# Attention beside a gated squared-ReLU block: `wo` and attention's output moved in transfers of 32 partitions, with waits between transfers taken from the kernel's own draft schedule

## Chip, core and metric

The kernel runs on one NeuronCore of a Trainium2 chip. The core has five engines that each run their own stream of instructions in order: TensorE (PE, matrix products; PEld is its weight load), VectorE (DVE), ScalarE (ACT), GpSimd (POOL) and SyncE (SP, which here only issues transfers). Transfers run on the 16 DMA engines that the profile counts for a core. The metric is the device time of one execution in microseconds.

## What is computed

`x` is 2048 tokens by 512, in float32. After a layer norm two branches start from the same `xn`, and are joined at the end:

```python
xn = _layernorm(x, axis=-1)
s = _A_ref(xn, A_wqkv, A_wo)                   # attention, then @ wo
g = _silu(_B_ref(xn, B_w1, B_b1, B_w2, B_b2))  # relu(xn @ w1 + b1)**2 @ w2 + b2
return x + s * g
```

Attention has 32 heads of 16 elements. Each token looks at 8 keys: its own and those 2, 4, ... 14 tokens before it; keys ahead of the first token are masked. `wo` is 512 x 512, `w1` 512 x 1792, `w2` 1792 x 512.

## The kernel before

**Numbers.** Every product is made of three float32r products: an operand is split into a high part (ACT writes `src` as float32r) and a low part (`src` minus the high part, on DVE or POOL), and high x high, high x low and low x high are added up in PSUM (`PASSES`, line 40; `split`, line 498). So behind each loaded weight stand one ACT operation and one subtraction before TensorE may use it.

**Stages.** First come the 16 tiles of 128 tokens: norm, transposition, and the products with `wqkv`. From the fifth tile on, the transposition is a shuffle of 32-partition blocks (`shuffle`, line 788: four transfers SBUF to SBUF, the rows `turn<-turn`) and a 32 x 32 transposition on DVE. q, k and v are staged in `stg` and stored to DRAM (`store_qkv`, line 930, into `sq`, `sk`, `sv`). Then the up products with `w1` run for both halves of the tokens (`ups`, line 1136; PE rows `uX`, `uY`, `uZ`). The second half's `u` goes to DRAM (`su`) and is fetched later (`load_ut`, line 1268). Last come the down products, in four chunks `c` of 512 tokens with 14 blocks `f` of 128 hidden units each. A block is 4 token tiles x 3 passes = 12 matmuls into the four PSUM tiles `pb`. `make_h` (line 1273) squares `u` on ACT into `h` and has the low part subtracted on POOL or DVE.

**Beside them.** DVE works through attention (`attention`, line 660) in eight units `u` of 256 tokens, whose 128 partitions are 16 blocks of 16 tokens by 8 groups of 4 heads. `load_u` (line 592) fetches q, k, v of a unit; `store` (line 654) writes the unit's output to DRAM, to `so`, laid out as 8 groups x 2048 tokens x 64 elements. In the down stage `load_o` (line 1320) fetches a unit back as `oq` with four heads' groups on 32 partitions, `trans_o` (line 1329) transposes 32 x 32 blocks on DVE into `oTf`, ACT writes the high part `oT`, `lowo` (line 1338) the low part, and `out_product` (line 1341) makes the 12 matmuls `pw<-wot,oT` of a tile. `finish` joins the branches and stores.

**Weights of the down stage.** During the first chunk (`c = 0`) the kernel fetches `w2` from block 6 on (`load_w2`, line 726, `split_w2`, line 730) and `wo` (`load_wo`, line 1371, two calls with two transfers each; `split_wo`, line 1377). `rwo`, the raw `wo`, and `oTf` share the two buffers of tag `rwo`.

**Order.** The kernel is traced twice. The first trace is a draft: a list scheduler (`forward`, line 219) lays all operations on the five engines with the kernel's own costs (`price`), transfers on one common wire of `RATE` bytes per ns, which SP may run `AHEAD` (2500 ns) of (line 61). It chooses the order on every engine, and whether an operation marked `E` goes to DVE or POOL. `arrange` (line 377) keeps the best of six rounds, and in the second trace fixes that order on each engine. So a change of a transfer also moves operations elsewhere. All transfers are issued by SP. Each signals one of eight DMA semaphores in turn, and waits for the transfer that had this semaphore before, eight transfers earlier, beside what its data need. A record of an operation is made in `add` (line 153), whose line 159 issues the instruction: the profile shows nearly all as L159 (L160 after the change), and operations are told apart by tile names.

Of the kernel before, what the change touches and what calls it, by code (L numbers as in the profile page):

```python
# [11 lines left out]
F32 = mybir.dt.float32  # L12
FR = mybir.dt.float32r
AF = mybir.ActivationFunctionType
# [3 lines left out]
P = 128  # L18
S = 2048
D = 512  # L20
# [10 lines left out]
UP = 256  # L31
NU = S // UP

GR = 8
CH = D // GR
BI = 16
NB = UP // BI
WIN = BI + HALO

PASSES = ((0, 0), (0, 1), (1, 0))  # L40
# [38 lines left out]
def elements(ap):  # L79
    n = 1  # L80
    for d in ap.shape[1:]:
        n *= d
    return n


class Book:
# [66 lines left out]
    def add(self, key, name, f, a, k):  # L153
        n = len(self.ops)
        engine = key
        if key == "E":
            engine = self.plan[1][n] if self.plan else "V"
            f = getattr(f[engine], name)
        ins = f(*a, **k)  # L159
        out = k["out"] if "out" in k else a[0]  # L160
        outs = [out] + ([k["accum_out"]] if "accum_out" in k else [])
        ins_ = [*(a if "out" in k else a[1:]), *(x for i, x in k.items() if i not in ("out", "accum_out"))]
        ins_ = [x for x in ins_ if isinstance(x, bass.AP)]
        two = sum(x.space != bass.MemoryType.PSUM and elements(x) > 1 for x in ins_) > (name != "tensor_scalar")
        if key == "E":
            op = Op(n, "E", ins, {e: self.price(e, name, k, ins_, out) for e in "VG"}, True)
        elif name == "dma_start":
            moved = 4
            for d in out.shape:
                moved *= d  # L170
            op = Op(n, "S", ins, 600, moved=moved)
        else:
            op = Op(n, engine, ins, self.price(engine, name, k, ins_, out),
                    engine == "V" and two or engine == "G" and elements(out) > 1 and name != "memset")
        if self.first:
            if op.engine in self.heads:
                self.heads[op.engine].starts.append(op)
                op.waits += 1
            self.heads[op.engine] = op
        func = next((x for x in a if isinstance(x, mybir.ActivationFunctionType)), None)  # L180
        op.table = func if func in (AF.Exp, AF.Silu) else None
        op.stream = self.in_stream
        self.ops.append(op)
        if engine == "P":
            if "P" in self.last:
                self.edge(self.last["P"], op)
            self.last["P"] = op
        for x, writes in [(x, False) for x in ins_] + [(x, True) for x in outs]:
            r = self.region(x)
            if r is None:  # L190
                continue
            t, p0, p1, m = r
            writes = writes or t.space == "PSUM"
            if t not in op.tiles:
                op.tiles.append(t)
                if not t.users:
                    used = self.firsts.setdefault(t.slot, [])
                    if len(used) >= t.bufs:
                        t.behind = used[-1]
                    used.append(op)  # L200
                if t.behind not in (None, op):
                    t.behind.starts.append(op)
                    op.waits += 1
                t.users.append(op)
            kept = []
            for other, w, q0, q1, k_ in t.log:
                if (w or writes) and other is not op and p0 < q1 and q0 < p1 and m & k_:
                    self.edge(other, op)
                if not (writes and p0 <= q0 and q1 <= p1 and k_ & ~m == 0):
                    kept.append((other, w, q0, q1, k_))  # L210
            kept.append((op, writes, p0, p1, m))
            t.log = kept
        return ins
# [138 lines left out]
    def tails(self, order=None):  # L352
# [21 lines left out]
        top = max(tail)  # L374
        return [top - t for t in tail]

    def arrange(self):
        if self.plan is None:
            order, best = None, None
            for _ in range(ROUNDS):  # L380
                end, order = self.forward(self.tails(order))
                if best is None or end < best[0]:
                    best = end, [op.n for op in order], [op.given for op in self.ops]
            return best[1:]
        order = [self.ops[n] for n in self.plan[0]]
        for op in self.ops:
            op.given = self.plan[1][op.n]
        for e in "PVAGS":
            line = [op for op in order if op.given == e]
            for a, b in zip(line, line[1:]):  # L390
                self.tc.add_manual_dep(b.ins.ins, a.ins.ins.name, mybir.DependencyInfo(
                    mybir.DependencyClass.NoSync, mybir.DependencyReason.DATA), reason="order")


class Kept:
# [47 lines left out]
def trace(ctx: ExitStack, tc: tile.TileContext, plan, x, wqkv, wo, w1, b1, w2, b2, out):  # L443
# [4 lines left out]
    PE, V, A, G, E = (Recorded(book, n, e) for n, e in zip(  # L448
        "PVAGE", (nc.tensor, nc.vector, nc.scalar, nc.gpsimd, dict(V=nc.vector, G=nc.gpsimd))))
    dma = Recorded(book, "S", nc.sync).dma_start  # L450

    def pool(name, stack=ctx, after=(), **k):
        return Pool(book, stack.enter_context(tc.tile_pool(name=name, bufs=1, **k)), name, after)

    const = pool("const")
    dram = pool("dram", space=bass.MemoryType.DRAM)
# [119 lines left out]
    sq = dram.tile([GR, S, CH], F32, name="sq")  # L576
    sk = dram.tile([GR, HALO + S, CH], F32, name="sk")
    sv = dram.tile([GR, HALO + S, CH], F32, name="sv")
    so = dram.tile([GR, S, CH], F32, name="so")
    sr = dram.tile([8, P, D], F32, name="sr")  # L580
    su = dram.tile([NF, P, 2, 512], F32, name="su")

# [9 lines left out]
    def load_u(what, u):  # L592
        n = BI if what == "q" else WIN
        src = dict(q=sq, k=sk, v=sv)[what]

        t = att.tile([P, n, CH], F32, name=f"{what}{u}", tag="k" if (what, u) == ("v", NU - 1) else what)
        row = src[0, u * UP:u * UP + 1, :]
        ap = bass.AP(tensor=row.tensor, offset=row.offset, ap=[[BI * CH, NB], [src.shape[1] * CH, GR], [1, n * CH]])
        dma(t.rearrange("p i c -> p (i c)"), ap)
        return t  # L600
# [52 lines left out]

    def store(u):
        v = tiles.pop(("v", u))
        row = so[0, u * UP:u * UP + 1, :]
        dst = bass.AP(tensor=row.tensor, offset=row.offset, ap=[[BI * CH, NB], [S * CH, GR], [1, BI * CH]])
        dma(dst, v[:, :BI, :].rearrange("p i c -> p (i c)"))

    def attention():  # L660

# [75 lines left out]
    mv, means, rs, shifts, xn, xb, pTs, seen, odd = ({} for _ in range(9))  # L737
# [291 lines left out]
    for a in range(2, NT, 2):  # L1029
        n, t = {2: 2, 4: 1}.get(a, 0), a + 2  # L1030
# [273 lines left out]
    p2 = pool("p2", ctx, (px, pstg, p2a, tpool))  # L1304
# [13 lines left out]
    oqs, oTs = {}, {}  # L1318

    def load_o(u):  # L1320

        if u in oqs:
            return
        oqs[u] = p2.tile([P, UP // 64, 2, 2, CH], F32, name=f"oq{u}", tag="oq")
        for g in range(GR):
            src = so[g, u * UP:(u + 1) * UP, :].rearrange("(b p e) c -> p b (e c)", p=32, e=2)
            dma(oqs[u][32 * (g // 2):32 * (g // 2) + 32, :, g % 2].rearrange("p b e c -> p b (e c)"), src)

    def trans_o(t):
        src = p2.tile([P, 512], F32, name=f"oTf{t}", tag="rwo", bufs=2)  # L1330
        src = src.rearrange("p (g n) -> p g n", g=4)
        V.transpose(out=src.rearrange("p (g h) (b n) -> p b g h n", h=2, n=32),
                    in_=oqs[t // 2][:, :, :, t % 2].rearrange("p b g (h c) -> p b g h c", c=32))
        oTs[t] = p2.tile([P, 2, 4, P], FR, name=f"oT{t}", tag="oT", bufs=3)
        A.activation(oTs[t][:, 0], src, AF.Copy)
        seen[t] = src

    def lowo(t):
        E.tensor_sub(oTs[t][:, 1], seen.pop(t), oTs[t][:, 0].bitcast(F32))

    def out_product(t, ps, cols=slice(0, D)):
        o = oTs[t]
# [26 lines left out]
    rwo = {}  # L1369

    def load_wo(i):
        rwo[i] = p2.tile([P, 2, D], F32, name=f"rwo{i}", tag="rwo", bufs=2)
        for g in range(2):
            row = wo[64 * i + 32 * g:64 * i + 32 * g + 1, :]
            dma(rwo[i][:, g], bass.AP(tensor=row.tensor, offset=row.offset, ap=[[P * D, 4], [D, 32], [1, D]]))

    def split_wo(i):
        for g in range(2):
# [14 lines left out]
    for c in range(NCH):  # L1393
        last = c == NCH - 1
        t0 = c * TPC
        for f in range(NF):
            if c == 0 and f in (2, 3):
                load_wo(f - 2)
# [25 lines left out]
            if f >= 7:  # L1424
                load_o(c * 2)
            if f in (9, 10) and not last:
                load_r(t0 + f - 9)
            if f == 11:
                for i in range(2):
                    trans_o(t0 + i)  # L1430
            if f == 12:
                for i in range(2):
                    lowo(t0 + i)
                load_o(c * 2 + 1)
# [18 lines left out]
        else:  # L1453
# [15 lines left out]
            for j in range(2, TPC):  # L1469
                n = D // 2 if j == TPC - 1 else D  # L1470
# [28 lines left out]
```

## Time and profile before

| | us |
|---|---|
| median of three runs | 477.09 |
| the three runs | 476.09, 477.09, 477.45 |
| the profiled execution | 475.35 |
| its span in the trace | 473.6 |

Durations below are from the profiled execution. Its own time is 1.75 us longer than the span that the trace shows. How the work lies over the span can be read from the slices of the page, 40 equal ones of 11.84 us, with the busy share in tenths. The weight loads (PEld) overlap with the matmuls, so the row of PE alone tells how full TensorE is.

```profile
PE   8999999999999999999999997999999999999996
...
DVE  4987977999999998999999984899999999992213
ACT  5756968866564558468584965795249535844311
POOL 2286324336997699956453567876674566376330
...
DMA  8799899999689977641860558748894994443102
```

The first slice holds the first loads and the warm-up. Slices 0 to 10 are the products with `wqkv`; the up products run to slice 22; the down stage starts in slice 22 with `c = 0`. Moved data are 87.78 MB in all.

### The profile page before, as it was taken

What the parts mean: (1) busy time and instruction counts of PE and PEld (TensorE: products, weight loads), DVE (VectorE), ACT (ScalarE), POOL (GpSimd) and SP (SyncE); (2) the same over time, 40 slices, a digit from 0 to 9 for tenths busy, and PEclk for the clock granted to TensorE, in tenths of its full rate; (3) what the DMA queues carried; (4) which work ended last, traced back from release to release, by engine and by line L of the source; (5) the groups of instructions that cost most, each with busy time, mean ns of one, the idle gap of its engine ahead of it and who ended that gap; (6) DMA issues with size and microseconds to landing.
All of it is one profiled execution on the core that took longest, in us unless ns stands there. A gap on an engine that the chain in (4) does not pass through costs nothing.

```text
span 473.6 us, 6218 instructions
## 1 busy us (share of the span) xinstructions
PE 463.6 (98%) x2037; PEld 380.6 (80%) x2037; DVE 403.9 (85%) x341; ACT 291.7 (62%) x567; POOL 280.5 (59%) x297
## 2 busy tenths in 40 slices
PE   8999999999999999999999997999999999999996
PEld 6788888888788888888888785788888888888886
DVE  4987977999999998999999984899999999992213
ACT  5756968866564558468584965795249535844311
POOL 2286324336997699956453567876674566376330
PEclk9999999999999999999999998999999999999999
DMA  8799899999689977641860558748894994443102
GB/s 276 210 219 280 287 220 285 253 230 252 184 226 275 261 239 201 227 105 47 209 155 2 156 144 205 193 124 251 174 255 115 259 238 142 146 144 91 45 19 72
DMA packets 77901, 87.78 MB, mean 185 GB/s; under 512 B 6956, under 2 KB 59436, under 8 KB 77868
## 3 DMA queue, kind: packets, MB, share of 16 engines
q1 hardware_dynamic: 77868, 87.38, 69.4%
q8 instruction: 16, 0.26, 0.2%
q14 instruction: 17, 0.14, 0.1%
HBM read 53.75 MB, written 30.47 MB: 178 GB/s over the span
## 4 chain that ended last, share of the span: by engine, by line
PE 89%; DMA 6%; POOL 1%; ACT 1%; DVE 1%; issue 1%; SPq 0%; POOLq 0%
PE pb L159 25%; PE uX L159 16%; PE pq L159 13%; PE pm L159 12%; PE pw L159 9%; PE uZ L159 8%; DMA w2r<-in_B_w 5%; PE uY L159 4%; DMA oq<-so 2%; PE warm L159 1%; SPq L159 0%; PE pxT L159 0%; POOL h L159 0%; DVE wq L159 0%; POOL w L159 0%
## 5 line engine op out<-in xcount | busy, mean ns | idle before, releaser
L159 PE MATMUL pb<-w,h 128*128 128x512 f32 x592 | 152.1, 394 | 3.6 <-POOL h L159 3.5
L159 PEld LDWEIGHTS pb<-w,h 128*128 128x128 f32 x592 | 111.6, 190 | 29.7 <-POOL h L159 5.8
L159 DVE TENSOR_TENSOR pr<-k,qp 128x2048 f32<-128x2048 f32 x32 | 72.8, 2276 | 7.3 <-ACT qp L159 5.6
L159 DVE TENSOR_REDUCE v<-pv 128x256 f32<-128x2048 f32 x32 | 73.0, 2281 | 0.7
L159 DVE TENSOR_TENSOR pv<-v,Lp 128x2048 f32<-128x2048 f32 x32 | 72.8, 2276 | 0.6
L159 DVE TENSOR_REDUCE L<-pr 128x128 f32<-128x2048 f32 x32 | 72.7, 2273 | 0.5
L159 POOL TENSOR_TENSOR h<-ut,h 128x512 fp32r<-128x512 f32 x26 | 33.3, 1295 | 34.6 <-ACT ut L159 33.3
L159 POOL TENSOR_TENSOR h<-u,h 128x512 fp32r<-128x512 f32 (+1 forms) x32 | 33.0, 1050 | 24.1 <-ACT u L159 16.8
L159 PE MATMUL pw<-wot,oT 128*128 128x512 f32 (+1 forms) x204 | 45.5, 376 | 0.0
L159 PEld LDWEIGHTS pw<-wot,oT 128*128 128x128 f32 x204 | 36.8, 188 | 7.1
L159 DVE TENSOR_TENSOR z<-z,pw 128x512 f32<-128x512 f32 (+1 forms) x17 | 11.0, 650 | 26.2 <-ACT z L159 14.4
L159 ACT ACTIVATE ut<-ut 128x512 f32<-128x512 f32 x42 | 24.8, 624 | 12.1 <-DMA ut<-su 12.0
L159 PE MATMUL pq<-wq,XA 128*128 128x512 f32 x122 | 31.5, 391 | 0.3 <-DVE wq L159 0.3
L159 ACT ACTIVATE u<-uX,b1t 128x512 f32<-128x512 f32 x28 | 19.2, 687 | 18.2 <-PE uX L159 14.6
L159 ACT ACTIVATE h<-ut 128x512 fp32r<-128x512 f32 x28 | 16.4, 625 | 22.3 <-PE pb L159 10.5
L159 POOL TENSOR_TENSOR u<-u,more 128x512 f32<-128x512 f32 x14 | 18.2, 1297 | 17.4 <-ACT more L159 16.7
L159 POOL TENSOR_TENSOR oT<-oTf,oT 128x512 fp32r<-128x512 f32 x16 | 20.7, 1295 | 11.3 <-ACT oT L159 11.3
L159 PEld LDWEIGHTS pq<-wq,XA 128*128 128x128 f32 x122 | 22.7, 188 | 5.4 <-DVE wq L159 0.7
L159 ACT ACTIVATE stg<-pm 128x512 f32<-128x512 f32 x30 | 18.0, 599 | 14.3 <-PE pm L159 12.0
L159 ACT ACTIVATE u<-u 128x512 f32<-128x512 f32 (+1 forms) x54 | 26.4, 528 | 0.2
L159 ACT ACTIVATE stg<-pq 128x512 f32<-128x512 f32 x24 | 14.3, 598 | 13.4 <-PE pq L159 10.8
L159 ACT ACTIVATE h<-u 128x512 fp32r<-128x512 f32 (+1 forms) x36 | 17.4, 528 | 5.9 <-PE pb L159 5.8
(166 smaller groups left out, 990.4 us busy)
## 6 DMA issues: line engine op xcount, KB each, us to landing
k<-sk SPq DMA_DIRECT2D x8, 960.0 KB
v<-sv SPq DMA_DIRECT2D x8, 960.0 KB, 7.1
su<-u SPq DMA_DIRECT2D x28, 256.0 KB, 2.5
ut<-su SPq DMA_DIRECT2D x28, 256.0 KB, 4.5
x<-in_A_x SPq DMA_DIRECT2D x16, 256.0 KB, 4.9
sk<-stg SPq DMA_DIRECT2D x8, 512.0 KB, 3.3
sq<-stg SPq DMA_DIRECT2D x8, 512.0 KB, 5.0
sv<-stg SPq DMA_DIRECT2D x8, 512.0 KB, 6.0
```

The source lines that it names most:

```text
L159: ins = f(*a, **k)
```

## The change

Four things change.

*Attention's output in DRAM.* `so` becomes 8 units x 32 x 8 groups x 512: a row holds half a block (`HB` = 8 tokens) of one group, 2 KB. `store` writes a unit in two transfers, one for each half of the blocks. `load_o` fetches a unit in four transfers of 32 partitions with two groups each, in place of eight of 32 partitions with one group each. The tokens then stand in `oq` in another order; `trans_o` puts `oTf` out in that order, and `positions` writes the high and low parts of `oT` back to the old one, with a step of 4 elements.

*`wo`.* `load_wo` fetches each half in four transfers of 32 partitions (2 x 512 elements on each), in place of two of 128 partitions (512 elements on each). The old pattern on the DRAM side is 4 x 32 x 512, the new one 32 x 2 x 512.

*Waits.* `landed` goes through the transfers in the draft's order. For each it looks for the latest transfer that has landed, by the draft, when this one starts; if that is a later one than any wait so far covers, the pair is put on a list, except for the operations of the first part of the program (`early`: up to the norm of tile 2). In the second trace `arrange` makes each pair a real dependency, so that SP waits for the earlier transfer before it issues the later one.

*The order*, as the scheduler makes it anew.

```diff
+HB = BI // 2
...
+        op.early = self.first
...
+    def landed(self, order):
+
+        out, line, last = [], [op for op in order if op.moved], -1
+        for i, op in enumerate(line):
+            done = max((j for j in range(i) if line[j].end <= op.start), default=-1)
+            if done > last and not op.early:
+                out.append((op.n, line[done].n))
+                last = done
+        return out
...
+        for n, m in self.plan[2]:
+            self.tc.add_manual_dep(self.ops[n].ins.ins, self.ops[m].ins.ins.name, mybir.DependencyInfo(
+                mybir.DependencyClass.Sync, mybir.DependencyReason.DATA), reason="landed")
...
-    so = dram.tile([GR, S, CH], F32, name="so")
+    so = dram.tile([NU, UP // HB, GR, HB * CH], F32, name="so")
...
-        row = so[0, u * UP:u * UP + 1, :]
-        dst = bass.AP(tensor=row.tensor, offset=row.offset, ap=[[BI * CH, NB], [S * CH, GR], [1, BI * CH]])
-        dma(dst, v[:, :BI, :].rearrange("p i c -> p (i c)"))
+        for i in range(2):
+            dma(so[u].rearrange("(b i) g n -> i b g n", i=2)[i], v[:, HB * i:HB * (i + 1), :].rearrange("p i c -> p (i c)"))
...
-        oqs[u] = p2.tile([P, UP // 64, 2, 2, CH], F32, name=f"oq{u}", tag="oq")
-        for g in range(GR):
-            src = so[g, u * UP:(u + 1) * UP, :].rearrange("(b p e) c -> p b (e c)", p=32, e=2)
-            dma(oqs[u][32 * (g // 2):32 * (g // 2) + 32, :, g % 2].rearrange("p b e c -> p b (e c)"), src)
+        oqs[u] = p2.tile([P, 2, UP // 64, 2, CH], F32, name=f"oq{u}", tag="oq")
+        for g in range(GR // 2):
+            dma(oqs[u][32 * g:32 * g + 32].rearrange("p g b e c -> p g (b e c)"), so[u, :, 2 * g:2 * g + 2])
...
-        src = src.rearrange("p (g n) -> p g n", g=4)
-        V.transpose(out=src.rearrange("p (g h) (b n) -> p b g h n", h=2, n=32),
-                    in_=oqs[t // 2][:, :, :, t % 2].rearrange("p b g (h c) -> p b g h c", c=32))
+        V.transpose(out=src.rearrange("p (g h b n) -> p b g h n", g=2, h=2, n=32),
+                    in_=oqs[t // 2][:, :, :, t % 2].rearrange("p g b (h c) -> p b g h c", c=32))
...
-        A.activation(oTs[t][:, 0], src, AF.Copy)
-        seen[t] = src
+        seen[t] = src.rearrange("p (g b n) -> p g b n", g=4, n=32)
+        A.activation(positions(t, 0), seen[t], AF.Copy)
+
+    def positions(t, a):
+        return oTs[t][:, a].rearrange("p g (n b) -> p g b n", b=4)
...
-        E.tensor_sub(oTs[t][:, 1], seen.pop(t), oTs[t][:, 0].bitcast(F32))
+        E.tensor_sub(positions(t, 1), seen.pop(t), positions(t, 0).bitcast(F32))
...
-        for g in range(2):
-            row = wo[64 * i + 32 * g:64 * i + 32 * g + 1, :]
-            dma(rwo[i][:, g], bass.AP(tensor=row.tensor, offset=row.offset, ap=[[P * D, 4], [D, 32], [1, D]]))
+        for g in range(4):
+            rows = wo[P * g + 64 * i:P * g + 64 * i + 64, :]
+            dma(rwo[i][32 * g:32 * g + 32], rows.rearrange("(h c) n -> c h n", c=32))
```

TensorE's order is the same before and after. Three places of the other engines' orders follow.

SP at the start of the down stage of `c = 0`, before. A row names the tile written, the tile read, and the shape; `w2r7` is the raw `w2` of block 7, `so` attention's output in DRAM, `v4` and `q6` are attention's inputs, `xr` the `x` that `finish` adds.

```order
L159 DMA w2r7_2780<-in_B_w2 128x512
L159 DMA so_155<-v3_1494 16x8x1024
L159 DMA w2r8_2819<-in_B_w2 128x512
L159 DMA rwo0_2816<-in_A_wo 128x1x512 x2
L159 DMA oq0_2939<-so_155 32x4x128 x8
L159 DMA rwo1_2841<-in_A_wo 128x1x512 x2
L159 DMA w2r9_2844<-in_B_w2 128x512
L159 DMA w2r10_2864<-in_B_w2 128x512
L159 DMA v4_1539<-sv_154 128x1x1920
L159 DMA w2r11_2885<-in_B_w2 128x512
L159 DMA q6_1565<-sq_152 128x1x1024
```

The same place now:

```order
L160 DMA w2r7_2788<-in_B_w2 128x512
L160 DMA v4_1543<-sv_154 128x1x1920
L160 DMA w2r8_2829<-in_B_w2 128x512
L160 DMA rwo0_2824<-in_A_wo 32x2x512 x4
L160 DMA oq0_2951<-so_155 32x1024 x4
L160 DMA rwo1_2851<-in_A_wo 32x2x512 x2
L160 DMA w2r9_2856<-in_B_w2 128x512
L160 DMA rwo1_2851<-in_A_wo 32x2x512 x2
L160 DMA xr0_2988<-in_A_x 128x512
L160 DMA xr1_3006<-in_A_x 128x512
L160 DMA w2r10_2876<-in_B_w2 128x512
L160 DMA w2r11_2897<-in_B_w2 128x512
```

`v4` has moved ahead of `w2r8`, the two `xr` ahead of `w2r10`; the store `so` of unit 3 now lies earlier (ahead of `w2r6`).

ACT in the same stretch, before; `wot` is the high part of `wo`, `w28` that of `w2`'s blocks 8 and 9, `h0_6` the high part of `h` for blocks 6 and 7 of `c = 0`, and `u03<-u03` squares in place for the low part.

```order
L159 ACTIVATE w28_2821<-w2r8_2819 128x512
L159 ACTIVATE wot_2750<-rwo0_2816 128x512 x2
L159 ACTIVATE qp5_2_1553<-q5_1520 128x512
L159 ACTIVATE u06_2607<-u06_2607 128x2x256
L159 ACTIVATE wot_2750<-rwo1_2841 128x512
L159 ACTIVATE h0_6_2869<-u03_2454 128x512 x2
L159 ACTIVATE u03_2454<-u03_2454 128x2x256 x2
L159 ACTIVATE w28_2821<-w2r9_2844 128x512
L159 ACTIVATE w210_2866<-w2r10_2864 128x512
L159 ACTIVATE wot_2750<-rwo1_2841 128x512
L159 ACTIVATE h0_8_2915<-u04_2589 128x512 x2
```

And now:

```order
L160 ACTIVATE w28_2831<-w2r8_2829 128x512
L160 ACTIVATE wot_2758<-rwo0_2824 128x512 x2
L160 ACTIVATE qp5_2_1557<-q5_1523 128x512
L160 ACTIVATE u06_2615<-u06_2615 128x2x256
L160 ACTIVATE h0_6_2881<-u03_2462 128x512 x2
L160 ACTIVATE u03_2462<-u03_2462 128x2x256 x2
L160 ACTIVATE w28_2831<-w2r9_2856 128x512
L160 ACTIVATE wot_2758<-rwo1_2851 128x512 x2
L160 ACTIVATE w210_2878<-w2r10_2876 128x512
L160 ACTIVATE h0_8_2927<-u04_2597 128x512 x2
```

The first `wot<-rwo1` has moved from ahead of `h0_6` to behind `w28<-w2r9`.

SP some 23 transfers into the program, with what each waits for, before. `x9` is a tile of `x`, `k0` attention's first input, `turn4` the shuffle of the first pair of tiles that needs one; a DMAHW name is one of the eight DMA semaphores.

```order
L159 DMA x9_391<-in_A_x 128x512 [waits DMAHW6_49,DVE_49]
L159 DMA k0_1331<-sk_153 128x1x1920 [waits DMAHW7_49]
L159 DMA turn4_337<-turn4_337 32x4x256 [waits DMAHW0_49,DVE_49,PE_49]
L159 DMA turn4_337<-turn4_337 32x4x256 [waits DMAHW1_49]
L159 DMA turn4_337<-turn4_337 32x4x256 [waits DMAHW2_49]
L159 DMA turn4_337<-turn4_337 32x4x256 [waits DMAHW3_49]
```

Now:

```order
L160 DMA x9_391<-in_A_x 128x512 [waits DMAHW6_49,DVE_49]
L160 DMA k0_1331<-sk_153 128x1x1920 [waits DMAHW7_49,DMAHW2_49]
L160 DMA turn4_337<-turn4_337 32x4x256 [waits DMAHW6_49,DVE_49,PE_49]
L160 DMA turn4_337<-turn4_337 32x4x256 x2
L160 DMA turn4_337<-turn4_337 32x4x256 [waits DMAHW3_49]
```

`x9` is the latest transfer that used DMAHW6 there, so the shuffle's first transfer now waits for `x9` to land; two of the four have no wait of their own left.

More of the change, by code (lines that the diff above doesn't have):

```diff
@@ L382, in arrange @@
                 if best is None or end < best[0]:
-                    best = end, [op.n for op in order], [op.given for op in self.ops]
+                    best = end, [op.n for op in order], [op.given for op in self.ops], self.landed(order)
             return best[1:]
```

## Prediction

> **What bounds the kernel now.** I read the busy shares first, then TensorE's rows in the timeline, then stages, and only then the transfers. TensorE is the bound: 98% of the span, while no other engine passes 85%.
>
> ```profile
> span 473.6 us, 6218 instructions
> PE 463.6 (98%) x2037; PEld 380.6 (80%) x2037; DVE 403.9 (85%) x341; ACT 291.7 (62%) x567; POOL 280.5 (59%) x297
> ```
>
> So only time in which TensorE stands still, or runs at a lower clock, can be won. The stages show where that is (columns: window, its length, TensorE's busy us and instructions, granted clock, DMA share, GB/s):
>
> ```profile
> 90.00:100.00 10.00, 10.00 (x45) 1.00 1.13 200
> ...
> 260.00:270.00 10.00, 9.91 (x45) 1.00 0.48 145
> 270.00:280.00 10.00, 9.78 (x43) 1.00 0.39 112
> 280.00:290.00 10.00, 8.29 (x30) 0.85 1.05 218
> 290.00:300.00 10.00, 8.71 (x38) 0.98 0.84 212
> 300.00:310.00 10.00, 9.71 (x42) 1.00 0.54 169
> ```
>
> A full window holds 45 or 46. From 260 to 310 some 30 matmuls are missing; this is the first 512 tokens' down product (`c = 0`), where `w2`, `wo` and attention's output are loaded. TensorE's timeline gives the size:
>
> ```profile
> 266.65 3.49 PE L159 MATMUL pb<-w,h 128*128 128x512 f32 x13
> ...
> 272.77 3.34 PE L159 MATMUL pb<-w,h 128*128 128x512 f32 x14
> ...
> 283.65 1.01 PE L159 MATMUL pb<-w,h 128*128 128x512 f32 x3
> 286.37 7.36 PE L159 MATMUL pb<-w,h 128*128 128x512 f32 x24 [1.71 <-POOL h L159]
> 295.02 2.79 PE L159 MATMUL pb<-w,h 128*128 128x512 f32 x11 [1.29 <-POOL h L159]
> ...
> 311.87 3.34 PE L159 MATMUL pw<-wot,oT 128*128 128x512 f32 x14
> 336.51 2.72 PE pb L159 x12
> ```
>
> The last row is from the chain: 12 matmuls in 2.72 us, 0.2267 each. The stage has 14 x 4 x 3 = 168, which need 38.08 us; it took 311.87 - 266.65 = 45.22. So **7.14 us are lost**. By parts: up to 272.77, 23 matmuls (5.21) in 6.12, 0.91 lost; up to 283.65, 48 in 10.88, none; then 3 (0.68) in 2.72, **2.04**; 24 (5.44) in 8.65, **3.21**; 70 (15.87) in 16.85, **0.98**. The 3.21 is more than its stop of 1.29, because the clock was halved after the first stop, as finer windows show:
>
> ```profile
> 266.00:267.00 1.00, 1.00 (x6) 1.00 1.01 293
> 269.00:270.00 1.00, 1.00 (x6) 1.00 0.27 97
> 278.00:279.00 1.00, 1.00 (x6) 1.00 0.19 66
> 279.00:280.00 1.00, 1.00 (x6) 1.00 0.31 115
> 288.00:289.00 1.00, 1.00 (x4) 0.50 1.15 269
> ```
>
> What ended the stops is POOL's `h`; behind it stands ACT, and behind ACT a transfer. ACT's timeline, then SP's, then the chain:
>
> ```profile
> 282.73 0.63 ACT L159 ACTIVATE wot<-rwo 128x512 fp32r<-128x512 f32 x1 [4.57 <-DMA rwo<-in_A_wo]
> ...
> 289.23 0.63 ACT L159 ACTIVATE w<-w2r 128x512 fp32r<-128x512 f32 x1 [3.80 <-DMA w2r<-in_B_w]
> 266.85 1.25 SPq L159 DMA_DIRECT2D rwo<-in_A_wo  x2
> 268.14 7.94 SPq L159 DMA_DIRECT2D oq<-so  x8
> 276.24 1.13 SPq L159 DMA_DIRECT2D rwo<-in_A_wo  x2
> 277.48 1.02 SPq L159 DMA_DIRECT2D w2r<-in_B_w  x2
> 277.48 11.73 DMA w2r<-in_B_w
> 292.51 9.93 DMA w2r<-in_B_w
> ```
>
> `wo` goes out at 266.85, and at 269 the DMA engines are 27% busy at 97 GB/s, where three microseconds before they did 293; at 278 and 279, after the second pair, it is 19% and 31%. About 4 of 16 engines work. The four transfers are 1 MB, at 97 to 115 GB/s some 9 to 11 us for these few engines. The `w2` rows issued behind them at 277.48 take 11.73 us, because part of each sits behind `wo`. ACT, in order, waits first for `wo` (4.57) and then for `w2` (3.80); `h` is queued behind both. By 291 the backlog also holds up the last `w2` rows (9.93), hence the 0.98.
>
> **The change, part by part.** (1) `wo`. The DRAM side of the old pattern begins with a dimension of 4, the new one with 32. I read the 27% as "as many engines as that dimension". The nearest rows for a transfer of 32 partitions are the shuffles `turn<-turn`, alone on the rings here:
>
> ```profile
> 94.00:95.00 1.00, 1.00 (x6) 1.00 1.16 147
> ```
>
> All engines work, but at 147 GB/s, SBUF to SBUF; the 2 KB rows from HBM at 266 had 293. So 1 MB takes between 3.6 and 7.1 us instead of about 10. I take the near end, since direction and row size are those of 266.
>
> The Trainium skill, page "DMA: Bandwidth & Descriptors", section "Why a DMA increments its semaphore by 16 and not by 1", says that a transfer runs on the largest number up to 16 that divides the slowest dimension of both its patterns, so 4 before and 16 after. The 27% agrees. The same page's "Rules for kernel authors" speak against this edit: most bandwidth with 128 partitions and 1 MiB or more, and disjoint partition parts serialize, so one transfer is better. By that rule the loads would gain nothing and the time would stay; here the 128-partition load is the one at 97 GB/s.
>
> Does everything then come in time? SP's new order puts `v4` (960 KB), `w2r8`, `wo`, `oq0`, `w2r9`, `xr0`, `xr1` ahead of `w2r10`: 960 + 256 + 512 + 512 + 512 + 256 + 512 + 256 KB = 3.87 MB from about 266.5. At 293 GB/s the last is through at 279.7, at the 218 of window 280 at 284.2, and lands up to 2 us later. ACT must split `w2r10` ahead of `h0_8` (0.63 + 1.14, then 1.3 on POOL), which TensorE wants 8 x 2.72 after 267.56, at 289.3: so it must land by 286.2. It holds at either end, at the slow one just. So 2.04 + 3.21 go, and with them the 0.98: **-6.23**. The 0.91 at the start stays: ACT is busy without a break there, and its order up to that place is the same:
>
> ```profile
> 261.00:278.00 17.00, 17.00 (x38) 1.00 0.48 140
> ```
>
> One half of `h0_1`'s subtraction moves to DVE, behind a product of 2.28 us; by DVE's place then this costs or wins up to 0.9, I take 0.
>
> (2) Attention's output. Stores go from 8 of 512 KB to 16 of 256 KB, loads from 64 of 64 KB to 32 of 128 KB with rows of 2 KB for 512 B. SP issues 20 fewer in all, and SP binds nothing. Transposes stay; `oT` is now written with a step of 4 elements. No ACT or POOL row shows such a write; on DVE one with a step of 2 (`pv`) costs what one without has (`pr`):
>
> ```profile
> L159 DVE TENSOR_TENSOR pr<-k,qp 128x2048 f32<-128x2048 f32 x32 | 72.8, 2276 | 7.3 <-ACT qp L159 5.6
> ...
> L159 DVE TENSOR_TENSOR pv<-v,Lp 128x2048 f32<-128x2048 f32 x32 | 72.8, 2276 | 0.6
> ...
> L159 POOL TENSOR_TENSOR oT<-oTf,oT 128x512 fp32r<-128x512 f32 x16 | 20.7, 1295 | 11.3 <-ACT oT L159 11.3
> ```
>
> I take 0; at double price 1.3 us on POOL per tile, hidden beside TensorE except for `oT0`, queued ahead of `h0_10`: at most +1.3.
>
> (3) The added waits. An SP wait holds every transfer behind it. The sharpest place is early: `turn4` now waits for `x9`, and behind it stand the stores of q, k and v.
>
> ```profile
> 21.74 2.92 SPq L159 DMA_DIRECT2D x<-in_A_x  x4
> ...
> 28.89 2.59 SPq L159 DMA_DIRECT2D turn<-turn  x4
> 37.27 1.32 DVE L159 STREAM_TRANSPOSE pxT<-turn 128x512 f32<-128x512 f32 x2 [3.45 <-DMA turn<-turn]
> x<-in_A_x SPq DMA_DIRECT2D x16, 256.0 KB, 4.9
> su<-u SPq DMA_DIRECT2D x28, 256.0 KB, 2.5
> ```
>
> `x9` goes out last of its four, near 24.3, and lands by the median 4.9 later, 29.2: `turn4` goes 0.3 later. The rings still hold `k0`'s 960 KB then, so its bytes move when they did. A wait costs only where the rings run dry; then by the lone `su` row 2.5 - 0.9 (256 KB at 293) = 1.6 us. Below nothing it can hardly be: order in the rings stays as issued. I take **+0.3**, with 0 and 3 as ends.
>
> What is late next? DVE, with attention; its last transposes and the product that needs them:
>
> ```profile
> 437.93 1.30 DVE L159 STREAM_TRANSPOSE oTf<-oq 128x512 f32<-128x512 f32 x2 [2.78 <-DMA oq<-so]
> 464.19 5.75 PE L159 MATMUL pw<-wot,oT 128*128 128x512 f32 x36
> ```
>
> 464.19 - 439.23 - 0.6 - 1.3 = 23 us of slack, of which the gain takes 6.
>
> Sum, against the profiled execution's own time: 475.35 - 6.23 + 0.3 = 469.4. That execution lies 1.74 below the median 477.09; I carry the difference over: 477.09 - 5.93 = **471.2**.
>
> **Rivals.** *Part of it* (0.12): `w2r10` or the ones after land behind 286, since `xr` now goes first; the clock drops again and the 3.21 stays. For it: the margin at 218 GB/s. Against: the 293 of 266. 477.1 - 2.04 - 0.98 = 474.1. *The split changes nothing* (0.10): four engines were not the cause, or 32 partitions load no faster, so the stops stay; 477.1. For it only the 147 of the shuffles; against it the 16 busy engines there. *Slower* (0.06): the added waits empty the rings in the first 130 us, where each of the six pairs of tiles needs a shuffle, a DVE transpose and a split before TensorE may go on. Price 1.6 us each, 9.6 in all: 477.1 - 5.9 + 9.6 = 480.8. It decides once the pairs lose over 7.4, five of six. Against it: DMA shares above 1 there (1.13 in window 90), so work is queued when a wait ends.
>
> **How the numbers follow.** My forecast, chance 0.72, has 470.0 (the 0.91 goes too and the waits cost nothing), or 468.8 if some of the 1.74 by which the other runs are longer comes from these same stops, to 473.5 (3 for the waits, or 1.3 for `oT0` and some of DVE's 0.9). With the part case the range goes to 475.6: **468.8 to 475.6**, leaving out 0.16 and some edges. About 0.3%, 1.43 us, is what a measurement of this kernel can tell from no change. Faster: 0.72 + 0.12 = 0.84, less 0.01 of spill, 0.83. Same: 0.10 and the spill, 0.11. Slower: 0.06.
>
> **What would show it.** Right: a DMA share near 1 just after `wo` goes out; `w2` rows landing in under 8 us; no ACT wait on `rwo`; no granted clock of 0.5; 168 matmuls in under 40 us. Wrong: a stop with `w2r` behind it near `h0_8`; TensorE idle before 266, ended by `stg`, XA or SA; an `oT` operation well over 1.3 us on POOL.

## The result, and the profile after

The changed kernel took 469.52 us (median of four runs, 469.12 to 470.2) where the kernel before, with a fourth run beside the three, took 477.27 (476.09 to 478.5): a ratio of 0.9839, 95% interval 0.981 to 0.9868. The prediction was 471.2, in a range of 468.8 to 475.6. The profiled execution took 469.87, span 468.1.

The page of the changed kernel first, busy time of each engine:

```profile
span 468.1 us, 6197 instructions
PE 460.5 (98%) x2037; PEld 379.1 (81%) x2037; DVE 403.5 (86%) x345; ACT 300.8 (64%) x569; POOL 281.5 (60%) x293
```

TensorE's share is 98% as it was: a share of the span could not show the gain, since the stops were a small part of it and the slow clock of 288 counted as busy. The stages show it (changed kernel; columns as in the prediction: window, length, TensorE's busy us and instructions, granted clock, DMA share, GB/s):

```profile
260.00:270.00 10.00, 10.00 (x45) 1.00 0.78 188
270.00:280.00 10.00, 10.00 (x46) 1.00 0.90 210
280.00:290.00 10.00, 10.00 (x46) 1.00 0.68 201
290.00:300.00 10.00, 10.00 (x46) 1.00 0.89 204
300.00:310.00 10.00, 10.00 (x46) 1.00 0.62 173
...
269.00:270.00 1.00, 1.00 (x6) 1.00 0.85 177
...
288.00:289.00 1.00, 1.00 (x6) 1.00 0.47 98
```

The five windows hold 229 matmuls in place of 198. At 269, where the DMA engines were 27% busy, they are 85% busy; at 288, where the clock was halved, it is 1.00. TensorE's timeline has the size of it, and something new:

```profile
266.22 3.34 PE L160 MATMUL pb<-w,h 128*128 128x512 f32 x13
...
304.70 5.60 PE L160 MATMUL pw<-wot,oT 128*128 128x512 f32 x24
...
359.10 3.11 PE L160 MATMUL pb<-w,h 128*128 128x512 f32 x13
364.32 3.34 PE L160 MATMUL pb<-w,h 128*128 128x512 f32 x14
371.41 2.79 PE L160 MATMUL pb<-w,h 128*128 128x512 f32 x11 [0.81 <-POOL h L160]
...
458.44 5.75 PE L160 MATMUL pw<-wot,oT 128*128 128x512 f32 x36
```

The first chunk takes 304.70 - 266.22 = 38.48 us where its 168 matmuls need 38.08: 0.40 lost, not 7.14. But from there to the last `pw` it is 458.44 - 304.70 = 153.74, and it was 464.19 - 311.87 = 152.32: 1.42 us are given back in later chunks, most of it at the stop at 371. ACT's timeline says how the first chunk got through:

```profile
275.47 1.15 ACT L160 ACTIVATE wot<-rwo 128x512 fp32r<-128x512 f32 x2
...
280.89 1.16 ACT L160 ACTIVATE wot<-rwo 128x512 fp32r<-128x512 f32 x2
285.00 0.63 ACT L160 ACTIVATE w<-w2r 128x512 fp32r<-128x512 f32 x1 [2.95 <-DMA w2r<-in_B_w]
```

ACT no longer waits for `wo` (it waited 4.57). It still waits 2.95 for `w2r10`, up to 285.00: that fits, with little to spare, since the next thing on ACT is `h0_8`, which TensorE asks for at about 266.22 + 8 x 2.72 = 288.

### The profile page after: what moved, and what is told of

Read it like the earlier page. It is cut to its first block, busy times and chain, and to the rows that moved or that the text cites. A ratio compares the mean times of both kernels' runs of the same rounds, so it can differ in the third digit from the quotient of the medians.

```text
span 468.1 us, 6197 instructions
## 1 busy us (share of the span) xinstructions
PE 460.5 (98%) x2037; PEld 379.1 (81%) x2037; DVE 403.5 (86%) x345; ACT 300.8 (64%) x569; POOL 281.5 (60%) x293
## 4 chain that ended last, share of the span: by engine, by line
PE 82%; DVE 6%; DMA 6%; ACT 3%; issue 2%; POOL 2%; SPq 0%; DVEq 0%; ACTq 0%; POOLq 0%
PE pb L160 21%; PE uX L160 16%; PE pq L160 13%; PE pm L160 12%; PE uZ L160 8%; PE pw L160 6%; PE uY L160 4%; DMA oq<-so 2%; DMA k<-sk 2%; DVE v L160 1%; DVE pv L160 1%; DVE L L160 1%; PE warm L160 1%; DMA xr<-in_A_x 1%; DVE pr L160 1%
## 5 line engine op out<-in xcount | busy, mean ns | idle before, releaser
L160 PE MATMUL pb<-w,h 128*128 128x512 f32 x592 | 149.9, 390 | 0.8 <-POOL h L160 0.8
L160 POOL TENSOR_TENSOR h<-ut,h 128x512 fp32r<-128x512 f32 x24 | 30.8, 1295 | 39.1 <-ACT ut L160 31.9
L160 POOL TENSOR_TENSOR h<-u,h 128x512 fp32r<-128x512 f32 (+1 forms) x29 | 29.8, 1045 | 20.8 <-ACT u L160 17.6
L160 POOL TENSOR_TENSOR oT<-oTf,oT 128x512 fp32r<-128x512 f32 x16 | 25.1, 1571 | 6.3 <-ACT oT L160 6.3
```

## The experiments

Four theories for the gain: A, the leading dimension of 4 in `wo`'s DRAM pattern kept it on four DMA engines; B, the new order on SP and ACT; C, the added waits; D, attention's larger transfers. The stage losses below are all worked out as above: from the first `pb` of the first chunk to its first `pw`, less 38.08.

**One pattern, nothing else.** `wo_lead128` keeps every instruction of the kernel before in its place.

```diff
-            row = wo[64 * i + 32 * g:64 * i + 32 * g + 1, :]
-            dma(rwo[i][:, g], bass.AP(tensor=row.tensor, offset=row.offset, ap=[[P * D, 4], [D, 32], [1, D]]))
+            dma(rwo[i][:, g], wo[P * (2 * i + g):P * (2 * i + g) + P, :])
```

> The kernel before, with one edit: the four wo transfers read 128 consecutive rows each, so their DRAM pattern is 128 x 512 in place of 4 x 32 x 512. Size, number, place and order of all transfers and instructions stay as before; which row of wo stands on which partition changes, so attention's projection is another one. Theory A (the leading dimension of 4 kept wo on four DMA engines, and the rest queued behind it): DMA share above 0.7 just after wo goes out, in place of 0.27; the stops of 1.71 and 1.29 us are gone; 470.0 to 472.0 us. Theory B (the new order on SP and ACT is what helps): 476 to 478, stops as before. Theory C (the added waits) and theory D (attention's larger transfers): the same, 476 to 478.

Measured: 468.59 us, ratio 0.982 (0.9803 to 0.9838). Its windows just after `wo` goes out, and TensorE's timeline:

```profile
269.00:270.00 1.00, 0.97 (x4) 1.00 0.87 281
270.00:271.00 1.00, 1.00 (x5) 1.00 0.96 297
```

```profile
267.42 3.50 PE L159 MATMUL pb<-w,h 128*128 128x512 f32 x13
271.36 0.73 PE L159 MATMUL pb<-w,h 128*128 128x512 f32 x2 [0.22 <-POOL h L159]
...
306.39 5.60 PE L159 MATMUL pw<-wot,oT 128*128 128x512 f32 x24
```

The share is 0.87 at 281 GB/s where it was 0.27 at 97, and 0.89 us are lost: the small loss at the start, which no part of `wo` touches. The time is below what A expected. The whole gain is in this one pattern; B, C and D are not needed for it. That the load has 128 partitions here and 32 in the changed kernel makes no difference that these runs show.

**The parts of the change alone.** `wo_only` is the kernel before with the new `load_wo`; `waits_only` is the kernel before with `landed`; `no_waits` and `o_only` are:

```diff
-        for n, m in self.plan[2]:
+        for n, m in ():
```

that is, the changed kernel without the waits, and for `o_only` with the old `load_wo` too.

> The kernel before with the new load_wo alone (four transfers of 32 partitions); the scheduler makes its order anew; no added waits, attention's output as before. Theory A: 469.5 to 472 us, no stop in the first chunk. Theories C and D: 476 to 478. Theory B says nothing here unless the order comes out as in the changed kernel.

> The kernel before with the added waits alone (the list landed, and the dependencies it makes); the draft's order stays as before. Theory A: wo still on four engines, the stops stay, 476 to 479 us (waits cost 0 to 2). Theory C (the waits pace the rings so that w2 is not queued behind wo): 470 to 473.

> The changed kernel without the added waits; the order on every engine stays as in the changed kernel. Theory A: no stop in the first chunk, 468 to 470.5 us. If the waits are also what makes the new stop of 0.98 us at 371 (they hold up attention's transfers, DVE runs late, ACT stands at qp behind it and POOL's h comes late), that stop is gone too: 468.0 to 468.7; if ACT's doubled oT writes make it, it stays: 469 to 470. Theory C: 474 or more.

> The changed kernel with the old load_wo and without the added waits, so attention's output alone; the scheduler makes its order anew. Theory A: the stops near 286 and 295 stay, 475.5 to 478.5 us. Theory D (fewer, larger transfers of oq free the rings): 470 to 473.

| | us | ratio to before, 95% | lost in the first chunk |
|---|---|---|---|
| `wo_only` | 469.22 | 0.9828 (0.9813 to 0.9843) | 0.91 |
| `waits_only` | 477.49 | 0.9999 (0.9988 to 1.001) | 8.59 |
| `no_waits` | 470.04 | 0.9842 (0.9825 to 0.9858) | 0.40 |
| `o_only` | 475.45 | 0.9953 (0.9937 to 0.9968) | 7.19 |

`wo_only` has all of the gain, as A said (0.28 below the range expected). The waits do nothing that can be measured, alone or in the changed kernel: C falls. `o_only` keeps the stops, as A said, though its median is just below the 475.5 expected: attention's part, with the order that comes with it, is worth 0.5% beside the old `wo`, and nothing that can be measured beside the new one. That half per cent has no place in the traces, since the two profiled spans are only 0.3 us apart; the profile of the kernel before is its fastest execution, so the traces can't show it, and it stays unexplained. The timeline of `waits_only` shows that the old stops only moved:

```profile
286.45 0.77 PE L159 MATMUL pb<-w,h 128*128 128x512 f32 x2 [2.40 <-ACT h L159]
288.89 8.03 PE L159 MATMUL pb<-w,h 128*128 128x512 f32 x24 [1.66 <-POOL h L159]
```

**The dose.** `lead4_after` and `lead2_after` have the changed kernel's plan (its order and its waits on every engine), and only in the executed program another pattern for the same four transfers; the second differs in the lines under the `if`:

```diff
-            dma(rwo[i][32 * g:32 * g + 32], rows.rearrange("(h c) n -> c h n", c=32))
+            dst, src = rwo[i][32 * g:32 * g + 32], rows.rearrange("(h c) n -> c h n", c=32)
+            if plan is not None:
+                half = 256 * (g % 2)
+                row = wo[64 * i + 32 * (g // 2):64 * i + 32 * (g // 2) + 1, half:half + 256]
+                dst = rwo[i][:, g // 2, half:half + 256]
+                src = bass.AP(tensor=row.tensor, offset=row.offset, ap=[[P * D, 4], [D, 32], [1, 256]])
+            dma(dst, src)
```

```diff
...
+                row = wo[256 * (g % 2) + 64 * i + 32 * (g // 2):256 * (g % 2) + 64 * i + 32 * (g // 2) + 1, :]
+                dst = rwo[i][64 * (g % 2):64 * (g % 2) + 64, g // 2]
+                src = bass.AP(tensor=row.tensor, offset=row.offset, ap=[[P * D, 2], [D, 32], [1, D]])
...
```

> The changed kernel with the order and the waits of its own draft, and four transfers for each half of wo as there, but each with a DRAM pattern that leads with 4 again (4 x 32 x 256, rows of 1 KB, 128 partitions). Theory A: DMA share near 0.25 to 0.35 where wo is alone, the stops are back, 474 to 479 us. Theory B (order) and theory C (waits): all else being that of the changed kernel, 469 to 471.

> As lead4_after, with four transfers of 64 partitions for each half whose DRAM pattern leads with 2 (2 x 32 x 512, rows of 2 KB). Theory A: DMA share near 0.13 and some 50 GB/s where wo is alone, 1 MB takes about 20 us, the stops are longer than with 4: 482 to 492 us. If the row length of 1 KB was what slowed lead4_after and not the leading dimension: 469 to 474.

Measured: 476.83 us with 4 (0.9986, 0.9968 to 1.0003), and 483.99 with 2 (a single run, beside 477.8 for the kernel before). Windows in which `wo` is nearly alone on the rings, of `lead4_after` and then of `lead2_after`:

```profile
276.00:277.00 1.00, 1.00 (x6) 1.00 0.27 90
277.00:278.00 1.00, 1.00 (x6) 1.00 0.28 96
```

```profile
277.00:278.00 1.00, 1.00 (x6) 1.00 0.13 49
...
281.00:282.00 1.00, 1.00 (x6) 1.00 0.13 49
```

4 of 16 is 0.25 and 2 of 16 is 0.125: the leading dimension, in engines, and some 24 GB/s for each. The rows were 1 KB in the one and 2 KB in the other, so their length is not the cause. With the order and waits of the changed kernel kept, the stops are back: 7.92 us lost with 4, 15.56 with 2. That rules out B. The largest of them in `lead2_after`:

```profile
300.17 1.22 PE L160 MATMUL pb<-w,h 128*128 128x512 f32 x2 [5.44 <-ACT h L160]
```

The Trainium skill, page "DMA: Bandwidth & Descriptors", section "Why a DMA increments its semaphore by 16 and not by 1", gives the rule: the largest number of engines up to 16 that divides the slowest dimension of both patterns. The shares of 0.13, 0.27 and 0.87 for leads of 2, 4 and 128 agree with it.

**The new stop.** At 371 POOL's `h` came late. Behind it stands ACT, which waits for DVE with `qp` (the query in PSUM, for which there is one buffer) and has `h` queued behind. Changed kernel, ACT and POOL:

```profile
367.76 0.60 ACT L160 ACTIVATE qp<-q 128x512 f32<-128x512 f32 x1 [3.37 <-DVE pr L160]
368.30 1.14 ACT L160 ACTIVATE h<-ut 128x512 fp32r<-128x512 f32 x2
...
370.09 1.27 POOL L160 TENSOR_TENSOR h<-ut,h 128x512 fp32r<-128x512 f32 x1 [3.17 <-issue]
```

and the same place of `wo_only`, with TensorE's start of that chunk:

```profile
360.01 3.11 PE L159 MATMUL pb<-w,h 128*128 128x512 f32 x13
...
365.57 0.60 ACT L159 ACTIVATE qp<-q 128x512 f32<-128x512 f32 x1 [1.83 <-DVE pr L159]
```

`qp` goes 8.66 us after the chunk's start (367.76 - 359.10) in the changed kernel, 5.56 in `wo_only`, which has no stop there. Two theories: the writes of `oT` with a step of 4 elements, which ACT does at nearly double price, or DVE, late by its own order and its waits for `oq` (attention's output, fetched back). Two kernels take the step off ACT; `after_again` is the changed kernel beside the first of them.

```diff
-        V.transpose(out=src.rearrange("p (g h b n) -> p b g h n", g=2, h=2, n=32),
+        V.transpose(out=src.rearrange("p (g h n b) -> p b g h n", g=2, h=2, b=4),
...
-        A.activation(positions(t, 0), seen[t], AF.Copy)
+        A.activation(oTs[t][:, 0], seen[t], AF.Copy)
```

```diff
-        return oTs[t][:, a].rearrange("p g (n b) -> p g b n", b=4)
+        return oTs[t][:, a].rearrange("p g (b n) -> p g b n", b=4)
```

The first is `step_dve` (DVE's transposition steps instead), the second `no_step` (nothing does).

> The changed kernel, with the step of 4 elements moved from the writes of oT (ACT and POOL) to DVE's transposition, which then writes oTf in the old order; the order and waits stay, since the draft's costs do not know of steps. ACT's oT operations should fall from 1.14 to about 0.62 us, POOL's from 1.55 to 1.30, and DVE's transpositions stay near 0.65, as the pxT rows with a step of 4 have. If ACT's doubled write makes the stop at 371: it is gone, 468.0 to 468.8. If DVE's lateness or the order makes it: it stays, 469 to 470.

> The changed kernel once more beside the three others on one chip, to compare step_dve with it: 469 to 470.5 us, the stop at 371 of 0.3 to 1.1 us, no stop in the first chunk. If the stop is not there in this profile, its size varies from run to run and only the times can tell.

> The changed kernel, with oT written without the step of 4 elements, so that the tokens of attention's output stay in another order than those of x (this part of the result is another one); order and waits stay. ACT's oT operation 0.63 in place of 1.14 us, POOL's 1.30 in place of 1.57, DVE's transposition 0.70. If the doubled writes make the stop at 371: it falls below 0.1 us, 468.3 to 469.0. If DVE's waits for oq and its order make it: 0.3 to 1.0 us remain, 469.3 to 470.3.

Measured: `step_dve` 470.65 us (469.59 to 473.06), `after_again` 470.2 (469.9 to 470.45), `no_step` 469.06 (468.87 to 469.77). The groups by shape (count | busy us, mean ns of one | idle before them), of the changed kernel, then `no_step`, then `step_dve`:

```profile
L160 POOL TENSOR_TENSOR oT<-oTf,oT 128x512 fp32r<-128x512 f32 x16 | 25.1, 1571 | 6.3 <-ACT oT L160 6.3
...
L160 ACT ACTIVATE oT<-oTf 128x512 fp32r<-128x512 f32 x16 | 17.9, 1135 | 5.0 <-PE pw L160 2.9 <-DVE oTf L160 2.1
L160 DVE STREAM_TRANSPOSE oTf<-oq 128x512 f32<-128x512 f32 x16 | 11.0, 699 | 4.9 <-DMA oq<-so 4.2 <-POOL oT L160 0.6
```

```profile
L160 ACT ACTIVATE oT<-oTf 128x512 fp32r<-128x512 f32 x16 | 9.9, 624 | 3.9 <-PE pw L160 3.3 <-DVE oTf L160 0.5
```

```profile
L160 DVE STREAM_TRANSPOSE oTf<-oq 128x512 f32<-128x512 f32 x16 | 17.3, 1099 | 4.4 <-DMA oq<-so 4.3
```

And the stop, in `no_step` and then in `step_dve`:

```profile
371.62 2.79 PE L160 MATMUL pb<-w,h 128*128 128x512 f32 x11 [0.61 <-POOL h L160]
```

```profile
373.29 4.17 PE L160 MATMUL pb<-w,h 128*128 128x512 f32 x11 [1.71 <-POOL h L160]
```

Without any step the stop stays, so ACT's doubled writes don't make it; the times alone would not tell, since the median of `no_step` lies between its two expected ranges (its profile is of its slowest run). With DVE's transposition 0.40 us longer the stop grows to 1.71, in a profile that is the slowest of five runs (the others took 469.59 to 471.58). (The expectation that DVE would step for nothing was wrong.) What the size of the stop follows is the time from the chunk's start to `qp`, in every kernel that has the changed kernel's order: 0.19 us at 8.01 (`no_waits`) and 0.18 at 8.01 (`lead2_after`), 0.48 at 8.32 (`after_again`), 0.59 at 8.42 (`lead4_after`), 0.61 at 8.44 (`no_step`), 0.81 at 8.66 and 1.71 at 9.84 (`step_dve`). So it hangs on when DVE gets there. DVE loses time at `oq`, as its timelines in the changed kernel and in `after_again` show:

```profile
330.48 0.71 DVE L160 STREAM_TRANSPOSE oTf<-oq 128x512 f32<-128x512 f32 x1 [1.48 <-DMA oq<-so]
```

```profile
330.92 0.71 DVE L160 STREAM_TRANSPOSE oTf<-oq 128x512 f32<-128x512 f32 x1 [3.11 <-DMA oq<-so]
```

`wo_only` has no wait there, `no_waits` has one of 2.25, and a stop: the added waits are not needed for it. Attention's part by itself does not make it either: `o_only`, which has that part under an order of its own, has no wait there, `qp` at 6.67 and no stop after the first chunk (152.32 from the first `pw` to the last, as in the kernel before). On its DVE, and on that of `wo_only`, this transposition stands one `pr` later:

```profile
339.15 2.27 DVE L160 TENSOR_TENSOR pr<-k,qp 128x2048 f32<-128x2048 f32 x1
341.35 0.70 DVE L160 STREAM_TRANSPOSE oTf<-oq 128x512 f32<-128x512 f32 x1
```

That is 29.82 us behind the first `pw` (311.53), where `oq` was there in the changed kernel 25.78 behind its own (330.48 - 304.70). This points to the order, which puts the transposition too early on DVE; no run moves that one operation alone, so it is not shown.

**A version that takes the good of both.** `wo_and_h1` is `wo_only`, with the one subtraction that the changed kernel's order had moved to DVE at the start of the first chunk put there by hand:

```diff
-        for u, (hi, lo) in parts:
+        for i, (u, (hi, lo)) in enumerate(parts):
...
-            E.tensor_sub(lo, u, hi.bitcast(F32))
+            (V if (c, f, i) == (0, 1, 0) else E).tensor_sub(lo, u, hi.bitcast(F32))
```

> The kernel before with the new load_wo, no added waits, attention's output as before, and the low part of the first half of h for block 1 given to DVE by hand (the changed kernel's scheduler did so by itself, and lost 0.31 us at the start of the first chunk where the kernel before and wo_only lost 0.9). Theory A with this second cause: nothing above 0.35 us is lost in the first chunk, 0.6 less than wo_only, 468.2 to 468.9 us. Rival: what TensorE wins there is lost again in a later chunk as the order changes: 469 to 470.5.

> wo_only once more beside the others on the same chip: 469 to 469.7 us, 0.9 us lost at the start of the first chunk, no stop in later chunks.

Measured: 468.75 us, ratio 0.9813 (0.979 to 0.9836), beside 469.21 for `wo_only_again` (0.982, 0.9799 to 0.9842). TensorE in the first chunk:

```profile
266.01 3.49 PE L159 MATMUL pb<-w,h 128*128 128x512 f32 x13
...
304.65 5.60 PE L159 MATMUL pw<-wot,oT 128*128 128x512 f32 x24
```

0.56 us are lost there, in place of 0.91: some of the expected 0.6, not all of it. It has the lowest median of the kernels with the whole computation, with no stop later, though its `qp` goes 8.84 us after the chunk's start: on its ACT the two `h` operations that follow `qp` in the changed kernel and in `wo_only` stand ahead of it. The intervals of this one, `wo_only` and the changed kernel overlap.

## The prediction, step by step

*What bounds.* Right. The chain from `wo` over `w2r` and ACT to POOL's `h` was read from the waits, and `wo_lead128` cut it at its first link alone.

*`wo` on four engines, -6.23.* Right in mechanism, and the dose confirms it. The stage gained 7.14 - 0.40 = 6.74. The difference of 0.51 comes from the 0.91 at the start, which was left standing on the ground that ACT's order stays. It went down to 0.40, for the larger part through DVE's half of `h0_1` (0.93 to 0.56 in `wo_and_h1`, beside `wo_only_again`), which the prediction had seen and put at 0, with 0.9 to either side. That this is not `wo` is shown by `wo_only` and `wo_lead128`, which lose 0.91 and 0.89.

*All lands in time, just.* `w2r10` was to land between 279.7 and 286; it landed at about 285.0. The slow end came out, but the sum counted bytes alone: SP spent 6.35 us on `oq0`'s four transfers (from 268.55) and came to `w2r10` only at 278.95, and at 274 the DMA share was 0.09.

*Attention's output at 0.* The step's price was wrong: an ACT write with a step of 4 elements costs 1135 ns for 626, a POOL subtraction 1571 for 1295, which the prediction had named as a sign of being wrong. The place was right: it is hidden beside TensorE, and `no_step` (0.982, 0.9795 to 0.9845) is not measurably faster than `after_again` (0.9844, 0.9821 to 0.9868).

*The waits, +0.3.* 0 by `waits_only`. The first shuffle went 1.16 us later in its profile (30.05 for 28.89) and 2.09 later in the changed kernel (30.98), more than the 0.3 worked out, and TensorE still saw nothing of it.

*What is late next.* Wrong in place. The slack of 23 us was taken at DVE's last transposition. DVE was late earlier, where ACT holds `h` behind `qp`; 1.42 us were given back there and at a smaller stop at 393. This is the step that failed: slack was checked at the end of a chain, and not at each engine that waits for DVE on the way. It was a term of +1.42 that the sum does not have.

*The rivals.* None came. No window of the first chunk has a lowered clock, the new pattern did end the waits for `wo`, and the added waits cost nothing that TensorE saw.

*The sum.* Against the profiled execution 469.4 was worked out and 469.87 measured. The spans differ by 5.5: -6.74 + 1.42 in the stages, TensorE 0.43 earlier at 126.01 (126.44 before), and 0.25 more behind the start of the last `pw`; the last two no part of the change explains. So the near hit on the profiled execution is in part luck: the 0.51 and the 0.43 won cover most of the 1.42 lost. (With 3 for the waits the forecast's upper end would be 473.9, not 473.5.) Against the median the prediction was 1.7 too high, by the 1.74 that was carried over from the one execution to the median. The stops themselves vary: `waits_only` lost 8.59 in the same stage in which the kernel before lost 7.14 in its profile, which was the fastest of its runs. Kernels with stops spread over 2 to 3 us (`waits_only` 476.41 to 478.41, `lead4_after` 475.74 to 478.95), those without over 0.5 to 1.4 (`wo_only` 469.06 to 469.59, `wo_lead128` 468.5 to 469.91), in fewer runs. So that distance seems to have gone with the stops, which is argued and not shown. The prediction had this as a lower edge (468.8) and not as its centre.

## What to carry to other kernels

When transfers are late while the DMA share is low, look at the first dimension of the patterns of the transfer that is alone on the rings: its share times 16 is the number of engines, and everything queued behind it on those engines waits with it. When a stop goes, ask at each in-order engine what now stands in front of the next thing needed, and take the variation that the stop made in the time to go with it.

## What the runs showed of the hardware

A transfer with a lead of 2 held 0.13 of the DMA engines' time at 49 GB/s, with a lead of 4 about 0.27 at 90 to 97 GB/s, and with 128 the rings moved up to 297 GB/s; four pieces of 32 partitions gave a kernel not measurably slower than two of 128 did (ratios of 0.9828 and 0.982 to the kernel before). A write with a step of 16 bytes into SBUF cost ACT 81% more (1135 for 626 ns) and DVE's 32 x 32 transposition 57% more (1099 for 699), while the same transposition with such a step into PSUM (`pxT<-turn`) takes 701 ns, as `oTf<-oq` does without one. Behind a stop of 1.71 us the granted clock fell to 0.50: in the kernel before behind 286, and in `step_dve` behind 373, where 11 matmuls took 4.17 us, for 2.79 in `no_step`:

```profile
375.00:376.00 1.00, 1.00 (x4) 0.50 0.43 140
```

Behind the stops of 1.29 us (before, at 295) and 0.81 us (changed kernel, at 371) it stayed at 1.00.
